# A windowed-attention and gated-MLP kernel: another way of unpacking float64 weights, split operands in the first unit, and a new order for the first units

## The chip, the cores and the metric

One core of one Trainium2 chip. The metric is the device time of one execution in microseconds. The core has a matrix engine (PE, with its weight loader PEld), three engines for element-wise work (DVE, ACT and POOL, that is VectorE, ScalarE and GpSimd) and SP, which here only issues transfers.

## What is computed

Inputs are q, k, v of shape (8, 8, 576, 64) in float32 and three weight matrices in float64, which reach the core as pairs of 32-bit words. A causal window of 64 keys is attended, the heads are joined to rows of 512, neighbouring rows are mixed with two vectors, and a squared-ReLU MLP with a sigmoid gate follows.

```python
scores = q @ k.T / sqrt(64);  mask: 0 <= i - j < 64
attn = softmax(scores);  x = heads joined of (attn @ v)        # (8, 576, 512)
xk = mu_k * x + (1 - mu_k) * x_prev;  xr = mu_r * x + (1 - mu_r) * x_prev
k = relu(xk @ w_k);  v = (k * k) @ w_v;  r = sigmoid(xr @ w_r)
out = r * v                                                    # w_k 512x1024, w_v 1024x512, w_r 512x512
```

## The kernel before

**Tiling.** The 4608 rows are cut into nine units of 512 rows. A unit has four attention groups g (two heads each, 128 partitions; g 0 to 3 belong to unit 0, g 4 to 7 to unit 1) and 80 products of a 128x128 weight block with a 128x512 operand: 16 for r (four columns m, four row blocks c), 32 for k, 32 for v. A product normally takes three matmuls, because both operands are split into a high and a low part in a reduced float32 format (`xs`, `ks` and `ws` are such pairs): high by high, high by low, low by high. A product with unsplit operands ("plain", tiles `xm` and `whole`) is one plain float32 matmul, which the trace shows as two records. `DIRECT = "rk"` makes the 16 r and 32 k products of unit 0 plain; all else is split.

**Attention of a group.** PE makes the scores; DVE masks them and takes the row minimum (`least`); ACT takes the exponential (`exp`, tile `pr`, with its sum read out by a second instruction); DVE inverts the sums (`shares`); `scale` multiplies; for the first four groups PE transposes (`flip`, against `ident`), ACT or DVE copies (`pt`), PE multiplies by v, and ACT or DVE copy the result to `xT`. `mix` then builds xr and xk: a scaled copy, a blend on DVE, and for split operands a cast (`high`) and a subtraction (`low`).

**Weights.** There are 20 chunks of 128x512 (w0 to w3 for r, w4 to w11 for k, w12 to w19 for v), each loaded as raw word pairs. `decode` (L390) turns a chunk into float32 and then into its two parts. Before, that is: ACT takes the absolute value of the upper word (`sign`), DVE or POOL clamps it, DVE shifts it, DVE puts the sign back (`top`), DVE puts in three bits of the lower word (`low`), then ACT or POOL casts (`first_part`) and POOL or DVE subtracts (`second_part`).

**Order.** Every step is a `Piece` with the engines it may run on. `play()` (L197) issues pieces in a simulated order, engine by engine, and each engine then runs its list strictly in that order, waiting at each instruction for its inputs. For about the first two units the order is a table written out by hand, `ORDER` (L81), one list of piece numbers per engine; after that keys and costs choose. Ahead of all of it POOL builds the constant masks (L325 to L338), and the first piece in its list is `band_mask` (L345). The helper `Engine` records every operation, so nearly all instructions carry line 165 in the profile (159 in the order of the changed kernel), and one goes by tile names.

## Time and profile before

| | before |
|---|---|
| median of 3 runs | 620.73 us (617.44 to 621.71) |
| span of the profiled execution | 620.3 us |
| PE busy | 603.7 us (97%) |
| DVE busy | 401.1 us (65%) |
| ACT busy | 375.4 us (61%) |
| POOL busy | 110.6 us (18%) |

A profile gives busy time per engine, the chain of work that ended last (followed back from the last instruction), and for each group of instructions what ended the idle time before it. PE stands at the top almost throughout, so the questions are how much work PE has, and when it first has enough to run without a gap. In the timeline a row gives start, duration, engine, operation, tiles and count; the spacing from one start to the next is what an instruction takes of its engine, and is a little less than the duration.

### The profile page before, as it was taken

How to read it: one execution, taken by the hardware profiler on the slowest of the kernel's cores; microseconds unless marked ns; L12 is line 12 of the kernel's file. 1: busy time of each engine (PE TensorE's matmuls, PEld its weight loads, DVE VectorE, ACT ScalarE, POOL GpSimd, SP SyncE). 2: the span in 40 equal slices, each digit the busy share in tenths (PEclk: the TensorE clock that was granted, in tenths of full speed). 3: DMA queues.
4: the chain of work that ended last, by engine and by line, in shares of the span. 5: the costliest groups of instructions: out<-in, count | busy, mean ns of one | idle time of the engine just before them, and what ended most of it. 6: DMA issues, size and time to landing. Idle time of an engine off the chain costs nothing.

```text
span 620.3 us, 18858 instructions
## 1 busy us (share of the span) xinstructions
PE 603.7 (97%) x7520; PEld 473.0 (76%) x7520; DVE 401.1 (65%) x1233; ACT 375.4 (61%) x1063; POOL 110.6 (18%) x180
## 2 busy tenths in 40 slices
PE   4899899999999999999999999999999999999997
PEld 3654478888888888888888888888888888888886
DVE  5899879956675568646872778286827583665211
ACT  5899876767366835673586457654766466734630
POOL 6533035102200122011300330023002300201000
PEclk9899899999999999999999999999999999999999
DMA  8887511522231323123321322133212221010001
GB/s 293 286 286 199 177 30 37 143 75 80 90 106 28 94 66 111 36 67 92 94 60 48 109 87 73 53 91 103 75 53 90 85 93 28 1 53 18 0 18 51
DMA packets 61014, 55.49 MB, mean 89 GB/s; under 512 B 10496, under 2 KB 54528, under 8 KB 60928
## 3 DMA queue, kind: packets, MB, share of 16 engines
q1 hardware_dynamic: 60928, 54.30, 28.7%
q8 instruction: 60, 0.98, 0.6%
q14 instruction: 26, 0.21, 0.1%
HBM read 44.83 MB, written 9.44 MB: 87 GB/s over the span
## 4 chain that ended last, share of the span: by engine, by line
PE 95%; DMA 2%; ACT 1%; issue 1%; SPq 0%; DVE 0%; ACTq 0%
PE bank L165 95%; DMA qk<-qT 1%; DMA raw<-w_r 1%; ACT pr L165 1%; DMA raw<-w_k 1%; SPq L165 0%; ACT wt L165 0%; DVE r L165 0%; ACT xm L165 0%; ACT th L165 0%; ACT pt L165 0%; ACT r L165 0%; DVE nmax L165 0%; ACTq L165 0%
## 5 line engine op out<-in xcount | busy, mean ns | idle before, releaser
L165 PE MATMUL bank<-xs,ws 128*128 128x512 f32 x1152 | 272.8, 396 | 0.0
L165 PEld LDWEIGHTS bank<-xs,ws 128*128 128x128 f32 x1152 | 215.9, 188 | 51.1
L165 PE MATMUL bank<-ks,ws 128*128 128x512 f32 x864 | 207.3, 398 | 0.0
L165 PEld LDWEIGHTS bank<-ks,ws 128*128 128x128 f32 x864 | 161.3, 188 | 39.9 <-issue 1.4
L165 DVE TENSOR_TENSOR ks<-kf,ks 128x512 fp32r<-128x512 f32 x71 | 52.9, 745 | 108.0 <-ACT ks L165 108.0
L165 ACT ACTIVATE pr<-pr,nmax 128x96 f32<-128x96 f32 (+1 forms) x288 | 105.0, 367 | 11.3 <-DVE nmax L165 10.6
L165 ACT ACTIVATE kf<-bank 128x512 f32<-128x512 f32 x72 | 42.9, 597 | 63.8 <-PE bank L165 63.8
L165 DVE CUSTOM_DVE_ANT_0 pr<-bank,bands 128x96 f32<-128x96 f32 x256 | 49.5, 250 | 15.7 <-PE bank L165 15.6
L165 ACT COPY xT<-bank 128x256 f32<-128x256 f32 (+1 forms) x38 | 13.3, 391 | 74.5 <-PE bank L165 74.0
L165 ACT ACTIVATION_READ_ACCUMULATOR pr<-pr,nmax 128x1 f32 x288 | 54.4, 189 | 0.0
L165 POOL CAST ks<-kf 128x512 fp32r<-128x512 f32 x7 | 4.3, 611 | 271.3 <-ACT kf L165 271.3
L165 PEld LDWEIGHTS bank<-pt,v 32*64 32x64 f32 (+1 forms) x3168 | 41.0, 131 | 12.5 <-issue 8.3
L165 PE MATMUL bank<-pt,v 32*64 32x96 f32 (+3 forms) x3168 | 44.1, 237 | 4.4 <-ACT pt L165 2.1
L165 ACT ACTIVATE kf<-kf 128x512 f32<-128x512 f32 x72 | 45.4, 631 | 2.1
L165 PE MATMUL bank<-xm,whole 128*128 128x512 f32 x96 | 44.9, 615 | 0.0
L165 DVE SCALAR_TENSOR_TENSOR r<-bank,r 128x512 f32<-128x512 f32 x36 | 24.5, 680 | 29.4 <-PE bank L165 29.4
L165 ACT ACTIVATE th<-bank 128x512 f32<-128x512 f32 x36 | 21.3, 591 | 35.8 <-PE bank L165 25.4
L165 ACT CAST ks<-kf 128x512 fp32r<-128x512 f32 x65 | 40.2, 619 | 2.0
L165 PEld LDWEIGHTS bank<-qk 64*32 64x32 f32 (+1 forms) x2112 | 28.4, 108 | 16.8 <-DMA qk<-kT 4.6
L165 PE MATMUL bank<-qk 64*32 64x96 f32 (+1 forms) x2112 | 33.4, 254 | 7.8 <-DMA qk<-qT 3.8
L165 ACT CAST xs<-d 128x512 fp32r<-128x512 f32 x52 | 31.3, 616 | 14.1 <-POOL d L165 11.8
L165 DVE TENSOR_TENSOR xs<-d,xs 128x512 fp32r<-128x512 f32 x60 | 38.7, 686 | 0.1
(79 smaller groups left out, 525.6 us busy)
## 6 DMA issues: line engine op xcount, KB each, us to landing
v<-v SPq DMA_DIRECT2D x128, 64.0 KB, 2.1
v<-v SPq DMA_DIRECT2D x128, 32.0 KB, 1.9
raw<-w_k SPq DMA_DIRECT2D x8, 512.0 KB, 6.1
raw<-w_v SPq DMA_DIRECT2D x8, 512.0 KB, 4.6
raw<-w_r SPq DMA_DIRECT2D x4, 512.0 KB, 5.5
outT<-r SPq DMA_DIRECT2D x8, 256.0 KB, 2.0
qk<-qT SPq DMA_DIRECT2D x8, 224.0 KB, 3.7
qk<-kT SPq DMA_DIRECT2D x8, 224.0 KB, 4.3
```

What stands on the lines that cost most here:

```text
L165: return lambda *args, **kw: tc.keep_in_program_order(op(*args, **kw))
```

## The change

Five edits. (1) `decode` has a new middle: `clamp` limits the upper word in place (POOL or DVE), `thirds` brings the top three bits of the lower word down in place (DVE by a shift, POOL or ACT by arithmetic on its top byte), `rebase` is one ACT pass with two slopes (Prelu) from the upper word to a bank of PSUM, and `join` is one DVE pass that shifts and ors. `sign`, `shift` and `top` are gone. (2) `DIRECT` is empty: unit 0's r and k products have split operands, so eight operands of unit 0 get a cast and a subtraction more, and all weights are split ahead of unit 0's use. (3) `scale` may run on ACT, as four activations with the inverse sums as scale. (4) `ORDER` is another table. (5) The planner's model of transfers differs, which acts through the order alone. `APART` is empty and changes nothing.

```diff
-DIRECT = "rk"
+DIRECT = ""
...
     "POOL": (
-        631, 520, 18, 11, 530, 553, 30, 22, 554, 47, 585, 565, 584, 1490, 34, 609, 618, 35, 87, 71, 632, 79,
+        611, 27, 32, 5, 510, 500, 16, 58, 57, 20, 51, 21, 10, 545, 1468, 54, 44, 612, 1470, 1471, 47, 55, 48, 79,
...
-        def sign(e):
-            words[n] = tmp.tile([P, WC], F32, name="wt", tag="tmp", bufs=TB)
-            sca.activation(words[n], raw[n][:, :, 1].bitcast(F32), AF.Abs)
+        def high():
+            return raw[n][:, :, 1].bitcast(F32)
 
         def clamp(e):
-            engines[e].tensor_scalar(words[n], words[n], HI_MAX, HI_MIN, op0=ALU.min, op1=ALU.max)
-
-        def shift(e):
...
-        def top(e):
...
-        def low(e):
+            engines[e].tensor_scalar(high(), high(), HI_MAX, -HI_MAX, op0=ALU.min, op1=ALU.max)
+
+        def thirds(e):
+
+            if e == "POOL":
+                pool.tensor_scalar(raw[n][:, :, 0], raw[n].bitcast(U8)[:, :, 3], 1 / 32, -31 / 64, op0=ALU.mult, op1=ALU.add)
+            elif e == "ACT":
+                sca.activation(raw[n][:, :, 0], raw[n].bitcast(U8)[:, :, 3], AF.Copy, scale=1 / 32, bias=-31 / 64)
+            else:
+                dve.tensor_scalar(raw[n][:, :, 0], raw[n][:, :, 0], 29, None, op0=ALU.logical_shift_right)
+
+        def rebase(e):
+
+            words[n, 0] = bank(WC)
+            sca.activation(words[n, 0], high(), AF.Prelu, scale=2.0**-112, alpha=2.0**32)
+
+        def join(e):
...
-            dve.scalar_tensor_tensor(words[n, 1].bitcast(U32), raw[n][:, :, 0], 29, words[n, 0],
-                                     op0=ALU.logical_shift_right, op1=ALU.bitwise_or)
+            dve.scalar_tensor_tensor(words[n, 1].bitcast(U32), words[n, 0].bitcast(U32), 3, raw[n][:, :, 0],
+                                     op0=ALU.logical_shift_left, op1=ALU.bitwise_or)
...
+                if e == "ACT":
+                    for o in range(G):
+                        sca.activation(pr[:, o], pr[:, o], AF.Copy, scale=rs[:, o:o + 1])
+                    return
                 engines[e].tensor_mul(pr, pr, rs.unsqueeze(2).to_broadcast([P, G, wide]))
```

Three places where the order moves. First ACT's list at the start of the program; `pr,sums<-pr,nmax` is an exponential, `wt<-raw` the old `sign`, `bank<-raw` the new `rebase`, `pr<-pr,rs` a quarter of a `scale`, and a cast to `ws` is a `first_part`. Before:

```order
L165 ACTIVATE pr,sums<-pr,nmax 128x128 x2
L165 ACTIVATE wt<-raw_148 128x512
L165 ACTIVATE pr,sums<-pr,nmax 128x128 x6
L165 ACTIVATE wt<-raw_153 128x512
L165 ACTIVATE pr,sums<-pr,nmax 128x128 x2
L165 CAST ws_269<-whole 128x512
```

and now:

```order
L159 ACTIVATE bank<-raw_143 128x512
L159 CAST ws_177<-wt 128x512
L159 ACTIVATE pr,sums<-pr,nmax 128x128 x8
L159 ACTIVATE bank<-raw_155 128x512
L159 ACTIVATE pr,sums<-pr,nmax 128x128 x7
L159 ACTIVATE bank<-raw_173 128x512
L159 ACTIVATE pr,sums<-pr,nmax 128x128
L159 COPY pt<-bank 128x512
L159 ACTIVATE bank<-raw_175 128x512
L159 ACTIVATE pr<-pr,rs 128x128 x4
```

The first exponential now stands behind a `rebase` and a cast of chunk w2 (tile raw_143), which SP now loads first of all, and `scale` has come to ACT.

Second, POOL's list from the end of `band_mask` (the eight selects on `bands`); a TENSOR_SCALAR on `raw` is a `clamp` or `thirds`, `wt<-wt` the old clamp, `pr<-pr,rs` a whole `scale`. Before:

```order
L165 AFFINE_SELECT bands_119<-bands_119 32x96 x8
L165 TENSOR_TENSOR pr_182<-pr_182,rs_185 128x512
L165 TENSOR_SCALAR wt_240<-wt_240 128x512
L165 TENSOR_TENSOR ws0_269<-whole_242,ws0_269 128x512
L165 TENSOR_TENSOR pr_193<-pr_193,rs_196 128x512
```

and now:

```order
L159 AFFINE_SELECT bands_117<-bands_117 32x96 x8
L159 TENSOR_SCALAR raw2_143<-raw2_143 128x512
L159 TENSOR_TENSOR ws2_177<-wt_171,ws2_177 128x512
L159 TENSOR_SCALAR raw0_155<-raw0_155 128x512
L159 TENSOR_TENSOR pr_179<-pr_179,rs_182 128x512
L159 TENSOR_TENSOR pr_204<-pr_204,rs_207 128x512
L159 TENSOR_SCALAR raw1_173<-raw1_173 128x512
L159 TENSOR_SCALAR raw5_175<-raw5_175 128x512 x2
```

The clamp of raw2_143, for which ACT's first `rebase` waits, is now the first thing behind the masks.

Third, PE around its first r product (`xm,whole` plain, `xs,ws` split; `pt,v` the values, `ident,pr` the flips, `qk` the scores of a later group). Before:

```order
L165 MATMUL bank<-pt,v 64x64 x16
L165 MATMUL bank<-ident,pr 128x128 x4
L165 MATMUL bank<-xm,whole 128x512 x5
L165 MATMUL bank<-pt,v 64x64 x16
L165 MATMUL bank<-ident,pr 128x128 x8
```

and now:

```order
L159 MATMUL bank<-qk 32x96 x32
L159 MATMUL bank<-pt,v 64x64 x16
L159 MATMUL bank<-ident,pr 128x128 x8
L159 MATMUL bank<-xs,ws_351 128x512 x9
L159 MATMUL bank<-pt,v 64x64 x16
L159 MATMUL bank<-xs,ws_351 128x512 x3
L159 MATMUL bank<-ident,pr 128x128 x8
```

In both lists `pt,v` x16 first is the values of group 1, then come flips of group 2 (both heads now; one head before, the other stands further up), the first r products, and the values of group 2. Five plain products, of two row blocks, have become three split ones of one row block and a fourth behind the values, and the scores of group 4 stand ahead of the first product instead of among the r products.

## Rows read from the trace of the kernel before

**Rows 1.** Chain that ended last, in order: start us, us, what, records.

```profile
21.40 21.36 PE bank L165 x217
...
65.73 1.93 issue
67.66 483.69 PE bank L165 x5154
...
616.71 0.69 DVE r L165
```

**Rows 2.** Page, costliest groups: busy us, mean ns, count of plain matmul records.

```profile
L165 PE MATMUL bank<-xm,whole 128*128 128x512 f32 x96 | 44.9, 615 | 0.0
```

**Rows 3.** PE's timeline: start us, duration us, operation, tiles, records.

```profile
26.03 4.46 PE L165 MATMUL bank<-xm,whole 128*128 128x512 f32 x10
30.42 1.15 PE L165 MATMUL bank<-pt,v 128*64 128x64 f32 x32
31.50 1.09 PE L165 MATMUL bank<-ident,pr 128*128 128x128 f32 x8
...
50.28 7.99 PE L165 MATMUL bank<-xm,whole 128*128 128x512 f32 x18
58.20 1.00 PE L165 MATMUL bank<-qk 64*32 64x96 f32 x64
...
211.50 14.21 PE L165 MATMUL bank<-ks,ws 128*128 128x512 f32 x60
225.64 2.41 PE L165 MATMUL bank<-pt,v 32*64 32x96 f32 x192
```

**Rows 4.** Two stretches: PE busy, granted clock (1.00 is full), DMA share, GB/s.

```profile
21.00:25.00 4.00, 3.60 (x42) 0.57 0.47 154
69.00:73.00 4.00, 4.00 (x28) 0.58 0.56 170
```

**Rows 5.** POOL's timeline, first 35 us.

```profile
5.34 2.52 POOL L165 TENSOR_SCALAR_AFFINE_SELECT bands<-bands 32x96 f32<-32x96 f32 x8
11.24 1.04 POOL L165 TENSOR_TENSOR pr<-pr,rs 128x512 f32<-128x512 f32 x1 [3.38 <-ACT pr L165]
...
17.32 0.61 POOL L165 TENSOR_SCALAR wt<-wt 128x512 f32<-128x512 f32 x1
...
31.18 1.29 POOL L165 TENSOR_TENSOR ws<-whole,ws 128x512 fp32r<-128x512 f32 x1
```

**Rows 6.** ACT's timeline, first 21 us.

```profile
5.39 0.40 ACT L165 ACTIVATE pr<-pr,nmax 128x128 f32<-128x128 f32 x1 [3.38 <-DVE nmax L165]
...
12.80 0.60 ACT L165 CAST ws<-whole 128x512 fp32r<-128x512 f32 x1
13.31 0.40 ACT L165 ACTIVATE pr<-pr,nmax 128x128 f32<-128x128 f32 x1
...
15.63 0.66 ACT L165 ACTIVATE wt<-raw 128x512 f32<-128x512 f32 x1
16.19 0.39 ACT L165 ACTIVATE pr<-pr,nmax 128x128 f32<-128x128 f32 x1
16.48 0.19 ACT L165 ACTIVATION_READ_ACCUMULATOR pr<-pr,nmax 128x1 f32 x1
...
20.79 0.56 ACT L165 COPY pt<-bank 128x512 f32<-128x512 f32 x1
```

**Rows 7.** Groups by form, DVE's decode passes: busy us, mean ns.

```profile
L165 DVE TENSOR_SCALAR bank<-wt 128x512 uint32<-128x512 uint32 x16 | 11.0, 689 | 0.2
L165 DVE TENSOR_SCALAR wt<-wt 128x512 f32<-128x512 f32 x11 | 5.1, 463 | 4.4 <-ACT wt L165 4.4
```

**Rows 8.** DVE and POOL timelines: passes that overlap, and one alone.

```profile
29.73 1.45 POOL L165 TENSOR_TENSOR pr<-pr,rs 128x512 f32<-128x512 f32 x1 [1.69 <-DVE rs L165]
...
31.53 1.49 DVE L165 TENSOR_TENSOR ws<-whole,ws 128x512 fp32r<-128x512 f32 x1
...
57.62 0.70 DVE L165 TENSOR_TENSOR ws<-wt,ws 128x512 fp32r<-128x512 f32 x1
```

## The prediction, made before the changed kernel ran

> **What bounds the kernel now.** I read the chain of work first. From 21.40 us on it is PE almost without a break, to 616.71; the only longer hole is 1.93 us at 65.73, put down to issue [rows 1]. So the time is: when PE first has work without end, plus how much work that is, plus holes, plus the 3.6 us from the last matmul to the end of the span (620.3 - 616.7). Then PE's own timeline for prices. Eighteen plain records take 58.20 - 50.28 = 7.92 us, 0.88 us for a product of two; sixty split matmuls take 225.64 - 211.50 = 14.14 us, 0.71 us for a product of three [rows 3]. There are 96 plain records, 48 products [rows 2]. Last the clock: after PE has stood still it runs at half the full rate for a while. Two stretches of 4 us have means of 0.57 and 0.58, so each lost 1.7 us: one behind the start-up waits, ahead of the first r product (26.03), one behind the hole at 65.73 [rows 3, 4].

> **What the change saves.** PE: 48 products at 0.88 - 0.71 = 0.173 us each, 8.3 us, all on the path. The hole at 65.73 lies inside the values of group 4, which follow the scores of group 7 directly; in the new list five products stand between them. I take it that the hole goes, with the slow stretch behind it: 1.9 + 1.7 = 3.6 us. If it stays, 3.6 us come back.

> DVE loses 20 shifts (0.41 to 0.69 us, most 0.69 [rows 7]) and 20 sign passes, and gains 11 `thirds` and two clamps. The new clamps and shifts step over every second word, which no row shows: between 0.46 (contiguous, in place) and 0.69 us (into PSUM) [rows 7]. I take 0.69, the price of the passes that read `raw` in the same steps. That is some 15 us of DVE work less, worth nothing by itself: PE doesn't wait for DVE in the chain. It pays for the split, which the 8.3 us need.

> The rest of the program: the planner now gives POOL 53 subtractions for `xs` instead of 4, and spreads `scale` over ACT and POOL. I cost this at nothing, since PE's 80 products a unit (57 us) cover it; a unit's seven subtractions at 1.29 us [rows 5] are 9 us of POOL. Without that cover a late `xs` would cost PE about the difference to DVE's 0.70 [rows 8] each.

> **What it costs: a later start.** ACT's list now begins with `rebase` of w2, then a cast. That `rebase` waits for POOL's clamp, and POOL builds masks until 5.34 + 2.52 = 7.86 us [rows 5]. With a clamp at about 0.6 us (contiguous: 0.61 [rows 5]; below) ACT starts at 8.5 instead of 5.39 [rows 6]. Behind `rebase` ACT's cast waits for DVE's `join`, 0.9 us with hand-offs, and the exponentials of group 0 are queued behind that cast, as DVE's minima are behind the `join`.

> From there I add up ACT's list to the last `scale` of group 2, for which the second flip in front of the first r product waits. 28 exponentials with their sums at 0.39 are 10.9 us; 16 quarter scales at 0.29 (an exponential without the sum, 16.19 to 16.48) 4.6; six `rebase` 3.4; two casts at 0.51 1.0; two copies at 0.56 1.1; one half copy 0.3 [rows 6]. Prelu on ACT has no row; I price it as the absolute value of the same words, 0.56 start to start [rows 6]. The order shows one table load in either program, so no switch is charged. Sum 21.3, and 8.5 + 0.9 + 21.3 = 30.7. With the flip at half clock (half of 1.09 [rows 3], doubled to 1.0 or not) the first split product starts at about 31.5 instead of 26.03. PE has by then done the scores of group 4 (1.0 us [rows 3]), which it had not before. Late by 31.5 - 26.0 - 1.0 = 4.5 us. POOL's own list to the split xr of row block 0 (seven clamps and `thirds` at 0.6, four subtractions at 1.29, two whole scales at 1.04 [rows 5], three casts, a copy and small ones) sums to 15 us behind 7.86, and with 5 to 6 us of waits for ACT's cast and for w1's `join` ends near 28.7, so 3 us are free there. SP now issues w2 ahead of q0 and k0; I price that at nothing, since the first minimum stands behind the `join`, which ends near 9.9.

> Behind the first product PE has four r products 2.8, the values of groups 2 and 3 2.2, the flips of group 3 0.9 and the scores of group 5 1.0: 6.9 us, all fed if the clock is full. PE stood still before, so I charge the 1.7 us of a slow stretch here. PE is then without end of work from 31.5 + 6.9 + 1.7 = 40.1.

> After that everything comes just in time. Two places, by the same prices. xr of row block 3 is cast after 34 us of ACT's list (34 exponentials, 24 quarter scales, ten `rebase`, 16 passes of about 0.53), at about 44 us, and is whole near 45; PE reaches it after eight products, at 45.8. w16 is cast after 73.5 us of it (59 exponentials, 32 quarter scales, 19 `rebase`, some 60 passes of 0.52): 8.5 + 0.9 + 73.5, 1.3 of waiting for the first r results, and a subtraction on POOL, 85.5. PE gets there after 57 products, three scores and a pair of values (2.4 [rows 3]): 40.1 + 40.3 + 2.9 + 2.4 = 85.7. With such margins some waits will show. From 0 (all hold) to 5 (a handful of collisions of 0.8 us, below); I take 2.0.

> **Sum.** 620.3 - 8.3 - 3.6 + 4.5 + 1.7 + 2.0 = 616.6 us. The profiled execution lies inside the runs of before (median 620.73), so I leave it so.

> [...] DVE's subtraction takes 0.70 us alone and took 1.49 while POOL had a subtraction in hand (31.18 to 32.47), and a `scale` on POOL took 1.45 instead of 1.04 [rows 5, 8]: 0.8 us for a collision. [...]

> **Rivals.**
> - *Everything holds.* No waits behind 40.1 and no slow stretch at 31.5: 616.6 - 2.0 - 1.7 = 612.9. For it: DVE has some 15 us less to do. Against it: PE does stand still while ACT works off its list, and the last time it did the clock fell. If DVE's clamps run at 0.46 it is likelier.
> - *DVE and POOL collide.* Between 10 and 65 us DVE has some 20 passes with two SBUF inputs, and POOL's list is over half full. If half meet at 0.8 us, DVE is 8 us later; it waits some 3 us for PE's flips anyway, so PE loses 5 beyond the 2.0 taken, near 621.6. For it: the rows above. Against it: before, DVE met POOL too, and PE lost nothing.
> - *POOL's word-stepping passes are dear (slower than before).* Seven clamps and `thirds` stand on POOL ahead of the first split operand, five more in the next 25 us, reading every second word or every eighth byte. From 0.6 us upwards each 0.1 us costs 0.7 us on that list; its 3 free us are used up at 1.0 us a pass. At the 1.29 us of a two-input pass [rows 5] PE is 2 us later still, 619; at about 2.2 us it is some 8 us later at the first product and 12 with the five others, 628, and beyond that slower. For it: no row shows such a pass, and the byte form is of another kind. Against it: the row nearest to it, one input, same size, is 0.61.

> **Chances.** My forecast (613.5 to 619.5) 0.46; everything holds (609 to 613.5) 0.24; collisions (619.5 to 626) 0.18; dear POOL passes (above 627) 0.12. A measurement of this kernel tells 1% from no change, 6.2 us: faster means below 614.5. That is the case that all holds and a fifth of my own, 0.34; slower is the last case, 0.12; within 1% 0.54. The range leaves out the dear passes at the top and the lowest part of the full gain: 611 to 624.

> **What would show it.** First exponential on ACT near 10.4 us, first `xs,ws` product near 31.5, PE without holes from about 40; 0.71 us a product from there; no hole of 2 us in the first values of unit 1; the end of PE near 613. Clamps on POOL of 0.6 us would take the slower rival away, 1.5 us and more make it. Wrong would be: PE first fed much before 30 us (ACT's list is not what it waits for), PE holes of over 5 us between 40 and 110 (collisions), or holes in later units (POOL's subtractions late).

## The result

The changed kernel takes 627.58 us (median of 4 runs, 627.14 to 627.86), the kernel before 620.33 (617.44 to 621.71): the ratio is 1.012 with a 95% interval of 1.0093 to 1.0146. It is slower by about 7 us, 0.9 to 1.5%, clear of no change. The prediction said 616.6 us. A single execution of the kernel before lay anywhere between 617.4 and 624.6 us over all runs of this study (618.9 on average where the mean granted clock was 0.999 or 1.00, 622.0 where it was 0.991 to 0.995), and its median moved from 619.9 to 621.0 between rounds of runs, so the ratios below, not single times, decide.

| | before | changed |
|---|---|---|
| median | 620.33 us | 627.58 us |
| span of the profiled execution | 620.3 us | 625.9 us |
| that execution's own time | not given | 627.67 us |
| PE busy | 603.7 us | 599.1 us |
| DVE busy | 401.1 us | 357.3 us |
| ACT busy | 375.4 us | 400.0 us |
| POOL busy | 110.6 us | 199.6 us |
| first r product | 26.03 us | 32.99 us |
| DVE's last pass starts (PE's last matmul ends 0.04 us earlier) | 616.71 us | 622.34 us |

First the timeline of PE in the changed kernel (start us, duration us, engine, operation, tiles, records; in brackets the idle time ahead and what the profile holds for its end). It answers to [rows 3].

```profile
31.36 1.97 PE L159 MATMUL bank<-ident,pr 128*128 128x128 f32 x8
32.99 3.35 PE L159 MATMUL bank<-xs,ws 128*128 128x512 f32 x9
...
38.15 1.04 PE L159 MATMUL bank<-ident,pr 128*128 128x128 f32 x8
42.45 1.65 PE L159 MATMUL bank<-qk 64*32 64x96 f32 x64 [3.27 <-DVE d L159]
44.03 1.78 PE L159 MATMUL bank<-pt,vs 128*64 128x64 f32 x32
45.74 16.54 PE L159 MATMUL bank<-xs,ws 128*128 128x512 f32 x70
62.58 4.22 PE L159 MATMUL bank<-xs,ws 128*128 128x512 f32 x17 [0.29 <-POOL xs L159]
...
69.54 5.38 PE L159 MATMUL bank<-xs,ws 128*128 128x512 f32 x22 [0.29 <-DVE ws L159]
75.36 4.46 PE L159 MATMUL bank<-xs,ws 128*128 128x512 f32 x18 [0.44 <-DVE wt L159]
...
87.75 2.50 PE L159 MATMUL bank<-pt,v 32*64 32x96 f32 x192 [2.44 <-ACT pr L159]
...
96.39 0.96 PE L159 MATMUL bank<-qk 64*32 64x96 f32 x60 [0.66 <-DMA qk<-kT]
```

The reader is to see two holes: 3.27 us in front of the scores of group 5, and 2.44 us in front of the first values of unit 1. Around the first one the clock is low as well. Two stretches of the same trace (PE busy, granted clock, DMA share, GB/s stand among the columns), beside [rows 4]:

```profile
28.40:35.20 6.80, 6.21 (x45) 5.49 (x46) 6.64 (x23) 6.77 (x25) 5.72 (x6) 0.50 0.48 145
42.00:45.50 3.50, 3.04 (x92) 2.80 (x94) 1.34 (x4) 0.00 (x0) 0.59 (x2) 0.51 0.22 77
```

The products themselves are as cheap as forecast: the 70 records behind 45.74 take 16.54 us, 0.71 us for a product of three. From about 97 us on PE works without a hole of more than 0.27 us to its end. So the products give the gain that was forecast, and what was lost was lost in the first 97 us.

The label on the hole of 3.27 us does not fit: DVE's `d` ended at 41.58, 0.87 us ahead of the scores, and they do not read it. What the scores do wait for (their q and k, and two banks) had all been there before 39.5. But there is one more instruction in front of them. Both kernels align the address of PE's next instruction in two places: ahead of the scores of group 5 (`MIDS = {5: 36}`, through `nc.tensor.addr_align(128, offset=MIDS[g])`) and ahead of the first values of every pair of groups (`offset=ALIGN`, 102). The gap is filled with NOPs, and their number depends on how many PE instructions happen to stand ahead. Such NOPs don't count as busy and stand in no view shown here, but the trace holds a record of each one in PE's queue. Their runs up to 130 us (the step is the median from one to the next; about every sixteenth takes longer, so a whole run comes to 73 to 76 ns a NOP):

```
         first to last NOP (us)   NOPs   step (ns)   what follows on PE
before      45.00 -  49.08          56      71       scores g5 at 49.26, 0.50 us of idle time ahead
            79.08 -  82.81          51      71       values g6, g7 at 84.27, none
           124.34 - 127.03          38      71       values g8, g9 at 128.62, none
changed     37.98 -  42.28          58      71       scores g5 at 42.45, 3.27 us of idle time ahead
            81.71 -  87.58          78      71       values g4, g5 at 87.75, 2.44 us of idle time ahead
            99.50 - 101.44          27      71       next values, none
```

In the kernel before, the queue began its 56 NOPs while PE was busy with the products ahead of these scores, and had 3.8 us of them left. Its timeline there:

```profile
40.77 7.99 PE L165 MATMUL bank<-xm,whole 128*128 128x512 f32 x18
49.26 1.09 PE L165 MATMUL bank<-qk 64*32 64x96 f32 x64 [0.50 <-ACT pr L165]
```

The fill cost 0.5 us at most. In the changed kernel PE had eight transposes left, about 1.2 us, and the rest of the 4.3 us was idle time. That is a theory so far; the runs below test it.

### The profile page after: what moved, and what is told of

Read it like the earlier page. It is cut to its first block, busy times and chain, and to the rows that moved or that the text cites. A ratio compares the mean times of both kernels' runs of the same rounds, so it can differ in the third digit from the quotient of the medians.

```text
span 625.9 us, 19088 instructions
## 1 busy us (share of the span) xinstructions
PE 599.1 (96%) x7568; PEld 483.6 (77%) x7568; DVE 357.3 (57%) x1127; ACT 400.0 (64%) x1159; POOL 199.6 (32%) x267
## 3 DMA queue, kind: packets, MB, share of 16 engines
q1 hardware_dynamic: 60928, 54.30, 28.4%
## 4 chain that ended last, share of the span: by engine, by line
PE 86%; DMA 5%; ACT 4%; SPq 2%; DVE 1%; issue 1%; ACTq 0%
PE bank L159 86%; SPq L159 2%; ACT pr L159 2%; DMA raw<-w_v 1%; DMA qks<-qT 1%; DMA v<-v 1%; ACT kf L159 1%; DMA raw<-w_r 1%; ACT bank L159 1%; DMA qk<-kT 0%; DVE raw L159 0%; DVE wt L159 0%; DVE r L159 0%; DVE pt L159 0%; DVE d L159 0%
## 5 line engine op out<-in xcount | busy, mean ns | idle before, releaser
L159 PE MATMUL bank<-xs,ws 128*128 128x512 f32 x1296 | 309.5, 397 | 1.1 <-DVE wt L159 0.4
L159 PEld LDWEIGHTS bank<-xs,ws 128*128 128x128 f32 x1296 | 243.2, 189 | 60.0 <-DVE wt L159 0.9
L159 DVE TENSOR_TENSOR ks<-kf,ks 128x512 fp32r<-128x512 f32 x69 | 50.6, 734 | 104.6 <-ACT ks L159 103.5
L159 POOL TENSOR_TENSOR xs<-d,xs 128x512 fp32r<-128x512 f32 x53 | 71.5, 1374 | 23.2 <-ACT xs L159 22.4
L159 POOL CAST ks<-kf 128x512 fp32r<-128x512 f32 x14 | 8.5, 613 | 165.4 <-ACT kf L159 165.3
L159 POOL TENSOR_TENSOR pr<-pr,rs 128x384 f32<-128x384 f32 (+1 forms) x30 | 32.8, 1103 | 66.0 <-DVE nmax L159 44.9
L159 DVE STREAM_TRANSPOSE pt<-pr 128x384 f32<-128x384 f32 x64 | 36.2, 573 | 15.9 <-ACT pr L159 9.6
L159 ACT CAST xs<-d 128x512 fp32r<-128x512 f32 x58 | 34.7, 617 | 16.0 <-POOL d L159 11.4
L159 ACT COPY xT<-bank 128x256 f32<-128x256 f32 (+1 forms) x35 | 11.9, 388 | 47.1 <-PE bank L159 47.1
L159 ACT ACTIVATE pr<-pr,rs 128x96 f32<-128x96 f32 (+1 forms) x108 | 31.3, 369 | 13.5 <-DVE rs L159 13.4
```

The costliest lines, as they stand in the source:

```text
L159: return lambda *args, **kw: tc.keep_in_program_order(op(*args, **kw))
```

## The experiments

Theory A is the fill: PE waits for its own NOPs. Theory B is the prediction's: ACT starts late (its first `rebase` waits for POOL's masks), and from there the operands come just in time, so that PE would have waited in any case. All ratios are against the kernel before.

**Take the first fill away.**

```diff
-MIDS = {5: 36}
+MIDS = {}
```

> The changed kernel without the alignment of PE's instruction addresses ahead of the scores of group 5 (the one entry of MIDS taken out). In the profiled execution of the changed kernel PE stands still from 39.2 to 42.45 us in front of these scores, and the trace's records of PE's queue hold 58 NOPs there, 71 ns apart, from 37.98 to 42.28; 78 more stand from 81.71 to 87.58, in front of the first values of unit 1, where PE stands still for 2.44 us. Without the first alignment the instructions behind it move up by 58, and the second one has some 8 to fill instead of 78. Theory A (the fill is what PE waits for): scores of group 5 start near 39.3, r products of row block 1 start when their xr is whole, near 43.2 instead of 45.74, the hole of 2.44 in front of the first values goes; 4 to 5 us less, 622.5 to 623.5 us. Theory B (ACT's late start and just-in-time operands set the time, the fill lies in time in which PE would wait anyway): within 1 us of the changed kernel, 626.5 to 628.

Measured: 624.54 us (6 runs, 624.26 to 624.80), ratio 1.0071 [1.0047, 1.0095]; 3.0 us less than the changed kernel. PE's timeline:

```profile
39.18 1.47 PE L159 MATMUL bank<-qk 64*32 64x96 f32 x64
...
41.66 16.53 PE L159 MATMUL bank<-xs,ws 128*128 128x512 f32 x70
...
82.53 1.80 PE L159 MATMUL bank<-pt,v 32*64 32x96 f32 x131 [0.89 <-ACT kf L159]
86.22 0.97 PE L159 MATMUL bank<-pt,v 32*64 32x32 f32 x53 [1.89 <-issue]
```

The hole in front of the scores of group 5 is gone, and the r products run on from 41.66 instead of 45.74: 4.1 us. Theory A holds there, and better than I expected (43.2). At the first values 1.0 us of it is lost again: the 78 NOPs are 8 now, but PE stops for 0.89 us behind eight matmuls, and for 1.89 us, put down to issue, behind 139. From the last product ahead of them to the end of the values it is 5.9 us here and 4.9 in the changed kernel. The second fill had covered two other waits. The products behind the stop ran slower: 21 records take 6.53 us, against 5.15 in the changed kernel.

**Make the first fill longer.**

```diff
-MIDS = {5: 36}
+MIDS = {5: 100}
```

> The changed kernel with the offset of the alignment ahead of group 5's scores moved from 36 to 100: 122 NOPs there instead of 58, and some 13 instead of 78 in front of the first values of unit 1. Theory A (the fill costs 72 ns a NOP behind the lead that PE's queue has): scores of group 5 start 64 x 0.072 = 4.6 us later, near 47.0; the first values have no hole of their own any more, so the end is 4.6 - 2.4, some 2 us later, 629 to 631 us. Theory B (PE would wait there anyway): scores at 42.5 to 44, and the time within 1 us, 626.5 to 628.5.

Measured: 631.07 us (630.79 to 631.38), ratio 1.0179 [1.0146, 1.0212]; 3.5 us more than the changed kernel. The trace holds 122 NOPs from 37.91 to 47.03, and PE's timeline shows:

```profile
47.21 1.65 PE L159 MATMUL bank<-qk 64*32 64x96 f32 x64 [8.41 <-issue]
```

64 NOPs more made the hole 5.1 us longer (3.27 to 8.41) and moved the scores by 4.76 us, to 47.21 where 47.0 was expected. PE does not use this time for anything: the dose decides for theory A. The end moved less than the scores did. It came out 0.1 us above the upper end of the range given.

**Let ACT start earlier.** One number of POOL's list moves; `band_mask` (611) is needed only by group 4.

```diff
-        611, 27, 32, 5, 510,
+        27, 611, 32, 5, 510,
```

> The changed kernel with one number of POOL's list moved: the clamp of w2 stands ahead of the band mask (2.5 us of POOL work, first needed by group 4's minima) instead of behind it. w2 lands at 4.13. Theory B (the late start on ACT is on the path): rebase of w2 near 6.4 instead of 8.98, first exponential near 8.4 instead of 10.90, first xs,ws product near 30.7 instead of 32.99, end 2 us earlier: 625 to 626 us. Theory A says the same of the first product, since the fill has a fixed length, and that the hole in front of group 5's scores stays at about 3.3 us. Rival C (transfers set the pace of the first 30 us: 370 to 400 GB/s from 9 to 27 us): first product still near 33, time unchanged, 627 to 628.

Measured: 624.98 us (5 runs, 623.36 to 625.58), ratio 1.0076 [1.0048, 1.0103]; 2.6 us less than the changed kernel. ACT's first `rebase` and PE's first r product and scores of group 5:

```profile
5.76 0.64 ACT L159 ACTIVATE bank<-raw 128x512 f32<-128x512 f32 x1 [0.26 <-POOL raw L159]
```

```profile
29.15 3.41 PE L159 MATMUL bank<-xs,ws 128*128 128x512 f32 x9
...
39.42 1.65 PE L159 MATMUL bank<-qk 64*32 64x96 f32 x64 [4.02 <-DMA raw<-w_v]
```

`rebase` moved from 8.98 to 5.76 and the first r product from 32.99 to 29.15. So the late start is on the path, as the prediction said, and transfers are not what sets these 30 us in this kernel (rival C falls here). The hole behind it stays, at 4.02 us: now it is put down to a transfer, which these scores don't wait for either.

**Both.**

> Both edits: no alignment ahead of group 5's scores, and w2's clamp ahead of the band mask. Theories A and B together: the sum of the two gains, 6 to 7 us, 620.5 to 621.5 us, about the kernel before. A alone (ACT's start not on the path): as e1_nopad, 622.5 to 623.5. B alone: as e3_earlyclamp, 625 to 626.

Measured: 620.83 us (10 runs, 618.66 to 622.51), ratio 1.0004 [0.9985, 1.0023]; 6.75 us less than the changed kernel, where the two alone gave 3.0 and 2.6. A and B each hold, and with both undone no difference from the kernel before is left that these runs can tell. The second stop in the first values is still there, and the clock falls behind it:

```profile
77.09 0.43 PE L159 MATMUL bank<-pt,v 32*64 32x96 f32 x8
78.41 1.80 PE L159 MATMUL bank<-pt,v 32*64 32x96 f32 x131 [0.89 <-ACT kf L159]
81.89 1.24 PE L159 MATMUL bank<-pt,v 32*64 32x32 f32 x53 [1.68 <-issue]
```

```profile
80.00:84.00 4.00, 2.32 (x69) 1.99 (x63) 1.67 (x6) 2.93 (x11) 2.01 (x7) 0.54 0.25 69
84.00:88.00 4.00, 4.00 (x12) 3.10 (x11) 2.58 (x6) 4.00 (x15) 2.22 (x2) 0.60 0.45 116
```

**What the stop named issue is.** The kernel before has one too, 1.93 us behind 75 of its first values [rows 1]:

```profile
64.54 1.18 PE L165 MATMUL bank<-pt,v 32*64 32x96 f32 x75
67.66 1.74 PE L165 MATMUL bank<-pt,v 32*64 32x96 f32 x117 [1.93 <-issue]
```

The alignment says where in the code these stops are: the values begin at instruction 102 of a 128, and a matmul is two instructions (one loads the weights: the trace of the kernel before has 7520 of each). 75 matmuls on, that is 102 + 150 = 252; 139 on, 102 + 278 = 380. Both are within four instructions of a multiple of 128 (256 and 384). And a packet of PE's own program (the profile's queue of kind instruction, 61 packets of 16 KB in the changed kernel, whose trace has 15576 records of PE's queue, 255 to a packet; 60 and 15448 in the kernel before, 257) starts within a microsecond of the start of each, 2.2 to 2.6 us ahead of its end (at 65.25 in the kernel before, 79.65 in e4_both). Theory D: PE gets its program in blocks of 256 instructions, and a run of small matmuls reaches the end of one block before the next has come. Theory E: an operand or a bank is late. Three kernels moved the code against the work. The first puts 16 NOPs more ahead of the values of e4_both:

```diff
-            tc.keep_in_program_order(nc.tensor.addr_align(128, offset=ALIGN))
+            tc.keep_in_program_order(nc.tensor.addr_align(128, offset=118 if g == 4 else ALIGN))
```

> e4_both with the first values of unit 1 aligned to offset 118 instead of 102: 23 or 24 NOPs in front of them instead of 8, and nothing else. In e4_both these values stop once more, 1.68 us after 139 of 192 matmuls, put down to issue, and 6.8 us at half the clock follow. Counted in PE's program, with two instructions for a matmul and the fill, the stop stands at a multiple of 256 instructions; the one in the kernel before (1.93 us after 75) stands at one too. Theory D (code loading: PE gets its program in blocks of 256 instructions, a block is asked for when the one before it is entered, and a dense run of small matmuls gets to the end of a block before the next is there): with 16 more in front, the block's start is passed before the operand wait that holds these values, so the stop of 1.68 us goes, and 1.7 to 3.4 us of slow clock with it: 616.5 to 619. Theory E (the stop is an operand or a bank that comes late, and has nothing to do with addresses): it stays, at the same place, 620.5 to 621.5.

Measured: 621.44 us (11 runs), ratio 1.0008 [0.9988, 1.0028]: no gain over e4_both, and a time where E put it. The stop did not go, but it moved:

```profile
78.70 1.66 PE L159 MATMUL bank<-pt,v 32*64 32x96 f32 x123 [0.89 <-ACT kf L159]
82.20 1.31 PE L159 MATMUL bank<-pt,v 32*64 32x32 f32 x61 [1.84 <-issue]
```

It stands behind 8 + 123 = 131 matmuls where it stood behind 139: eight matmuls earlier for 16 NOPs, so at the same address. As an operand's wait it would have stayed at the same matmul, as the wait of 0.89 us behind eight matmuls did. The place speaks for D; my reckoning of when the block is asked for, on which the cure rested, was wrong.

The second does the like to the kernel before:

```diff
-MIDS = {5: 36}
+MIDS = {5: 36, 7: 4}
...
-            tc.keep_in_program_order(nc.tensor.addr_align(128, offset=ALIGN))
+            tc.keep_in_program_order(nc.tensor.addr_align(128, offset=8 if g == 4 else ALIGN))
```

> The kernel before with its code moved and nothing else: an alignment ahead of the scores of group 7 (some 31 NOPs) and the first values of unit 1 aligned to offset 8 instead of 102. Theory D: the block that the scores of group 7 begin in is entered some microseconds earlier, during the products in front, so the next one is there when the values reach it: the hole of 1.93 us at 65.73 goes, and the slow stretch behind it (1.7 us): 616.5 to 618 us. Theory E, or what the prediction took the hole for (values directly behind scores): the hole stays, 620 to 621 us or more.

Measured: 622.10 us (11 runs), ratio 1.0029 [1.0009, 1.0049]: a little slower, not faster. Instead of one stop there are two:

```profile
62.67 1.15 PE L165 MATMUL bank<-pt,v 32*64 32x96 f32 x58
66.48 2.50 PE L165 MATMUL bank<-pt,v 32*64 32x64 f32 x127 [2.66 <-issue]
70.38 0.48 PE L165 MATMUL bank<-pt,v 32*64 32x64 f32 x7 [1.40 <-issue]
```

They are 127 matmuls apart, 254 instructions, with a wait or two between them one block of 256. Theory E has no reason for that distance. A count of all of PE's records in the trace settles the place: ahead of the six stops seen in five kernels (before, e1_nopad, e4_both, e5_code118, b1_code) stand 1473 of them (twice) or 1729 (four times), and 1729 less 1473 is 256. The 0.89 us wait stands at 1465 in e4_both and at 1481 in e5_code118, so it does not keep to an address. Again the cure failed, though: PE entered the block before at 60.37, and the packet for the next one started only at 64.18, after PE had stopped.

The third and fourth give the block time, by moving products in between. In the kernel before, three products move from behind the first values to in front of them (the fill there is set to one or two NOPs):

```diff
-        1565, 1543, 1566, 742, 689, 690, 1572, 1567, 1580, 1588, 1589, 1590, 1573, 1591, 1574, 1575, 1596,
+        1565, 1543, 1566, 742, 1572, 1567, 1580, 689, 690, 1588, 1589, 1590, 1573, 1591, 1574, 1575, 1596,
```

> The kernel before with three products of unit 0 (six matmuls, 2.6 us) moved from behind the first values of unit 1 to in front of them, behind the scores of group 7; the first values' alignment is set so that it fills one or two NOPs. b1_code showed two stops 127 matmuls (254 instructions) apart in these values. Theory D: the block that the values stop for has 2.6 us more to come, the hole of 1.93 us goes with its slow stretch of 1.7 us: 617 to 618.5 us, and the spread of the runs (618 to 623.6 so far) narrows. This is what the prediction took the new order to do. Theory E: hole stays, 620 to 621.

Measured: 620.96 us (11 runs, 619.63 to 622.18), ratio 1.0012 [0.9997, 1.0028].

```profile
66.58 2.41 PE L165 MATMUL bank<-pt,v 32*64 32x96 f32 x192
...
82.53 2.49 PE L165 MATMUL bank<-pt,v 32*64 32x96 f32 x192 [2.09 <-issue]
```

The first values run through, as D has it, and the products behind them are not slowed: 14 plain records take 6.28 us, 0.45 each, where the 20 behind the stop in the kernel before took 10.35, 0.52 each. But the next values, which had no hole before, now have one of 2.09 us, in front: the same alignment as ever stands there, with 51 NOPs as before, and PE comes to it with less work in hand (1.7 us behind the first NOP, where it was over 5). So the time stayed above D's range. The spread did narrow.

In e4_both three products move between the values of group 4 and of group 5:

```diff
-        1604, 669, 670, 1612, 1622, 1623, 1613, 1614, 1624, 1595, 752, 1596, 1597, 1615, 1605, 1606, 1625, 1607,
+        1604, 669, 1612, 1622, 1623, 670, 1613, 1614, 1624, 1595, 752, 1596, 1597, 1615, 1605, 1606, 1625, 1607,
```

> e4_both with three k products of unit 0 (nine matmuls, 2.1 us) moved from behind the first values of unit 1 to between the values of group 4 and those of group 5; no work is added or taken. e5_code118 showed that the stop in these values keeps its place in the code (16 NOPs more in front, 8 matmuls earlier) but does not go by a shift of the code. Theory D (a block of PE's program comes late behind a dense run of small matmuls, 3.6 to 3.9 us from entering one block to having the next): the three products give the load 2.1 us, the stop of 1.7 us and the 6.8 us at half clock behind it go, 616.5 to 618.5 us. Theory E (operand or bank late): the stop stays, or stands in front of the moved products; 620 to 622.

Measured: 619.81 us (11 runs, 619.12 to 620.34), ratio 0.9978 [0.9965, 0.9991]: a little faster than the kernel before, 7.8 us less than the changed kernel.

```profile
79.64 0.97 PE L159 MATMUL bank<-ks,ws 128*128 128x512 f32 x3
81.56 1.68 PE L159 MATMUL bank<-ks,ws 128*128 128x512 f32 x6 [0.95 <-DVE wt L159]
83.17 1.31 PE L159 MATMUL bank<-pt,v 32*64 32x96 f32 x96
```

```profile
80.00:84.00 4.00, 3.05 (x83) 2.05 (x84) 0.69 (x1) 2.39 (x10) 2.04 (x7) 1.00 0.23 66
```

The stop is gone, the clock stays at full (1.00 where e4_both has 0.54), and another wait, of 0.95 us, shows instead. It is put down to DVE's `join` (`wt`), which PE doesn't read; what it was is open, but it does not stand at a block's end (1649 records ahead). The median is 1.3 us above the range that D gave.

**Three more, for ACT's list and the products in between.** In e5_code118, one of the two `scale` steps of group 2 (piece 565) moved from ACT to DVE:

> e5_code118 with one of the two scale steps of group 2 on VectorE (0.7 us behind a copy) instead of ScalarE (four quarters, 1.2 us). ScalarE's list is what the second flip of group 2, and with it the first r product, waits for (theory B): first r product some 0.8 us earlier, end 0.5 to 1 us earlier than e5_code118. If VectorE's list is as full as ScalarE's there: unchanged or up to 0.7 us later.

Measured: 623.03 us (11 runs), ratio 1.0044 [1.0029, 1.0058], slower than e5_code118. In the profiled execution the first r product stands at 30.50 (30.00 in e5_code118):

```profile
26.97 1.98 PE L159 MATMUL bank<-pt,v 128*64 128x64 f32 x32 [2.80 <-DMA v<-v]
...
79.59 2.36 PE L159 MATMUL bank<-pt,v 32*64 32x96 f32 x184 [0.89 <-ACT kf L159]
```

DVE did the scale in time: both scales of group 2 were done by 27.03, in e5_code118 by 28.9. But PE stood until 26.97 for a load of v, issued at 20.29, that the values of group 1 ahead of these flips need. So the time was no longer ACT's, and it was not a full list on DVE either. This execution is the fastest of the eleven (619.87 us; the others took 622.34 and more), and it has no stop in the first values, though the code is that of e5_code118. What differs is the packet: it started at 77.44, 0.8 us ahead of these values, in e5_code118 at 79.83, 2.5 us behind their start. It also rules out a late `join` as the cause of the stop: the values ran through to 81.95 while that `join` ended at 82.70 (in e4_both it ended at 81.50, 0.4 us before the stop did).

e7_between with two products between instead of three:

> e7_between with two products instead of three between the values of group 4 and of group 5: the third waited there 0.95 us for an operand from VectorE (w13). Theory D: two products (1.4 us) with the 0.9 us operand wait in front are nearly enough for the block to come: the wait of 0.95 goes, a stop of 0 to 0.6 us may come back; 619 to 620.3 us, and if a stop is long enough for the clock to fall, 2 to 3 us more in those executions.

Measured: 619.54 us (12 runs, 618.59 to 619.98), ratio 0.9976 [0.9962, 0.9990]. The wait of 0.96 us stayed (the second product has it too), no stop came back. With e7_between, from which these runs don't tell it apart, it is the fastest version here, 8.0 us below the changed kernel and some 0.2% below the kernel before. Then three `thirds` passes taken off ACT's list and given to POOL (pieces 72, 93, 142) in e8_two:

> e8_two with three of ScalarE's thirds passes (w7, w10, w17; 0.56 us each, start to start) given to GpSimd (0.7 us each), which has idle time there. Theory B (ScalarE's list is what the operands of 55 to 85 us come from, just in time): the waits of PE there (0.5 on xs, 0.3 on ws, 0.4 and 0.9) shrink by up to 1.1 us together, 618 to 619. If GpSimd's subtractions are late instead: PE's wait on xs near 54 grows from 0.5 to 1 us and the time is that of e8_two or above.

Measured: 621.15 us (12 runs), ratio 1.0006 [0.9986, 1.0026]; 1.6 us more than e8_two. PE's wait on `xs` shrank from 0.54 to 0.42 us, but new ones came 5 us later:

```profile
59.74 1.06 PE L159 MATMUL bank<-qk 64*32 64x96 f32 x62 [0.82 <-DVE nmax L159]
61.70 12.28 PE L159 MATMUL bank<-xs,ws 128*128 128x512 f32 x45 [0.91 <-ACT kf L159]
```

Neither of the two outcomes I gave fits. ACT's load alone is not what sets these operands. What was late in its place is not shown.

## Why the prediction was wrong

**The ledger.** The forecast put the end of PE at 613.0 us; it came at 622.3, 9.3 us later. 1.5 us stand ahead of the first r product (32.99 for 31.5). 4.15 lie between it and the last products without end (45.74 - 32.99 = 12.75 us for 8.6): 3.27 of fill and the other 0.9 about what the half clock cost beyond the 1.7 charged, since the clock was low for 5.7 of these 12.75 us (28.4 to 35.2 and 42.0 to 45.5 in the trace). 3.7 lie behind 45.74: the labelled holes there sum to 4.4 us, against 2.0 allowed, 2.44 of them the second hole; the other 1.3 have no label and are not explained. Outside the span another 1.8 us (below). Together 11.1; the median missed by 11.0.

**The step that failed** is "6.9 us, all fed if the clock is full. [...] PE is then without end of work from 31.5 + 6.9 + 1.7 = 40.1". In the changed kernel it was so only from 45.74. I listed r products, values, flips and the scores of group 5 with their durations, and left out an instruction that stands in the code ahead of these scores, in both kernels: the alignment, whose 58 NOPs held PE for 3.27 us. The kernel before had the same fill at the same place with 56 NOPs, so no row showed it as a cost: it lay under eight microseconds of products. The change moved the scores of group 5 to a place where PE has 1.2 us of work in hand. The number of NOPs follows from a count of PE's instructions in the program, so it could have been had before any run.

**"I take it that the hole goes."** The 1.93 us at 65.73 were taken to come from values right behind scores. That was near the cause (a dense run of small matmuls, at the end of a block of code), and right that products in between take the stop away (b2_between, e7_between); but the new order also moved the code, and the fill of 78 NOPs took its place. With the fill gone the stop was back, 1.89 and 1.68 us. Not before e7_between was an order found in which the stop and the slow clock behind it go, and of the 3.6 us no more than 1.0 to 1.6 showed in the time (620.83 to 619.81 us; 1.0004 to 0.9978), since other waits came in their place.

**The products.** 0.71 us each: right. From 37.18 to the end of PE e4_both takes 578.2 us; less its labelled holes there (4.0) and half of the 5.3 us in which PE worked at half clock (2.6) that is 571.6; the forecast had 570.9 (572.9 less 2.0).

**The later start.** Right in kind and nearly in size: first exponential 10.90 (10.4), the scales of group 2 done at 31.6 (30.7), first r product 32.99 (31.5); the rest is the flip at half clock (1.97 us for the eight records at 31.36, at a granted clock of 0.50; 1.04 for the eight at 38.15, at 1.00). e3_earlyclamp shows that it is on the path, with 2.6 us for one moved number. What I did not ask is whether POOL had to build that mask first.

**The prices without a row.** Clamps on POOL measured 0.64 to 0.71 us (0.6 forecast), the byte form of `thirds` 0.67 to 0.73, `rebase` 0.61 to 0.66, as forecast for an absolute value. DVE's in-place passes were cheaper than both bounds when alone (0.42 us, some 0.34 from start to start), but three beside POOL's subtractions and cast took 0.90, 0.83 and 1.50:

```profile
29.33 3.07 DVE L159 TENSOR_SCALAR raw<-raw 128x512 f32<-128x512 f32 x3
...
39.40 0.42 DVE L159 TENSOR_SCALAR raw<-raw 128x512 f32<-128x512 f32 x1
```

So these passes, with one input, took two to four times as long beside POOL's work as alone; what the two engines contend for is not shown. The rival of collisions had counted passes with two inputs only. PE did not wait for these three.

**SP's list** was priced at nothing, and that was an oversight rather than a finding: SP stood from 38.7 to 44.20 at the load of group 7's k, which waits for the scores of group 5, with six weight chunks behind it. It was late because the scores were late: with the fill gone, in e4_both, the load goes out at 36.22, and PE's timeline shows no wait for a load from 37 us on.

**The base.** The sum was made against the profiled execution's span, 620.3 us, and left so. Every profiled execution here whose own time is known shows 1.7 to 2.2 us between that time and its span, mostly 1.8 (627.67 and 625.9; 620.78 and 619.0). So that execution of the kernel before, whose mean clock is 0.994, took about 622 us, one with the stop in it, and 616.6 should have read 618.4.

**The rivals.** None of the three happened. The slower one gave 628 and the time came to 627.6, but its mechanism, POOL's passes at 2.2 us, is false: the size agreed by chance. Collisions cost PE at most 1.0 us, the holes on `xs`, `ws` and `wt` between 62 and 76, not the five of the rival. "PE holes of over 5 us between 40 and 110" was the sign I gave for collisions; the holes came and were something else.

## What to carry to other kernels

When a change moves PE's instructions, count them: an alignment's fill, and the blocks in which the program is loaded, move with the code. Here the fill cost 0.5 us at most where PE had 3.8 us of work in hand behind its queue, and 3.27 us where it had 1.2; the stops put down to the blocks took 1.4 to 2.7 us each. Where the profile's releaser of a hole is an instruction whose result is not read there, or is issue, look at what stands in the queue itself before looking for a late operand. And when an engine's first work waits for another's set-up (here 2.5 us of masks), ask which of that set-up is needed first.
